# Query sketches on 16 tiles of 32 by 32, half of the first v on ScalarE's queue, five weight casts on GpSimd, and the last 256 queries taken with batch 3

## The chip, the cores and the metric

The kernel runs on one core of a Trainium2 chip. The metric is the device time of one execution in microseconds; the time before is 104.08 us, the median of three runs (103.90 to 104.26). The engines of the core are TensorE (PE; its weight loads are shown apart as PEld), VectorE (DVE), ScalarE (ACT), GpSimd (POOL) and SyncE (SP, which here only issues transfers). All follow fixed instruction orders and wait for each other by semaphores.

## The reference

Two stages follow each other. The first is an attention whose softmax is replaced by a polynomial sketch, for 4 batches, 4 heads, 1088 positions and a head width of 32, with r = 8; the second is a gated feed-forward network (FFN) over 4352 tokens of width 128 with 1536 hidden units.

```python
def phi(x):
    a = np.einsum('rd,bhsd->bhsr', S1, x)
    b = np.einsum('rd,bhsd->bhsr', S2, x)
    return np.einsum('bhsi,bhsj->bhsij', a, b).reshape(*x.shape[:-1], r * r)
q_p, k_p = (phi(q), phi(k))
kv = np.einsum('bhsf,bhsd->bhfd', k_p, v)
z = np.sum(k_p, axis=2)
num = np.einsum('bhsf,bhfd->bhsd', q_p, kv)
den = np.einsum('bhsf,bhf->bhs', q_p, z)[..., None] + 1e-06
x = num / den            # then heads are put side by side: 4352 x 128
gate = np.maximum(x @ w_gate, 0.0)
out = gate * (x @ w_val) @ w_out
```

## The kernel before

**Tokens.** A batch's 1088 positions are 34 columns of 32 tokens. Eight blocks of four such columns (NX = 8) make 1024 tokens; the two columns left over in each batch make one last set of 256 tokens over all four batches. A vector transpose (L1003) turns q into qT, with head and head width on the 128 partitions.

**Keys, class K, once per batch.** kT (L495), the sketches of the keys in TensorE (L502: two groups of 64 rows by four of 32 columns, weights wS, which ScalarE makes at L334), their transposes (L513), the outer products kp on GpSimd (L555; for the first batch one of five pieces on VectorE), z (L528), its masked copy zs (L536), and w (L542), which is z multiplied with S2, so that the denominator of a query needs only a third sketch. ScalarE copies w from PSUM (L547). v is cast to 16 bits by ScalarE (L561); L568 multiplies kp with v, and L575 writes the masked result bz.

**Queries, class Q, in sets.** The sets are: the first 256 tokens of batch 0 (a path of its own, in token order), the next 768 of batch 0, 1024 tokens each of batches 1, 2 and 3, and the last 256. For all but the first, `sk1` (L694) computes the sketches by S1 and S2 of two heads at a time into two PSUM banks, and `sk2` (L701) the third sketch by w into the second half of the first bank. `t2` (L708) and `t2c` (L714) transpose both into SBUF. Small products, a sum and a reciprocal follow (L741, L747, L752, L772). The class G then makes the outer products qqp (L835, on GpSimd), transposes them on TensorE (L853, copied by L858 or L860) or by a transfer (L843), multiplies with bz (L869) and writes xT (L881).

**FFN, class F.** A unit is 512 columns of a gate product (L926), a value product (L938), a relu by ScalarE (L931), a product on VectorE (L948), every sixth one on GpSimd (L943, L953), and the output product (L960), which sums over 12 units of a group of 512 tokens in one bank. Groups follow in the order of the query sets. Weights arrive as nine thirds of 256 KB in fp32 in the buffers of later k, q and v, and are cast to 16 bits by ScalarE (L412) or GpSimd (L414); the dictionary CAST says which.

**Order.** The function issues the early transfers by hand: S1 and S2 on ScalarE's queue, everything else on SyncE's, in the order k0, q0, v0 (four loads of one fourth each), weights, k1, q1. The rest is ordered by a planner (class Plan): each operation has an engine, an estimated cost, what it comes after, the PSUM banks it takes and drops (a Lease of one bank or of two neighbouring ones) and a due time; LAND holds estimated landing times, T0 + u * U the due time of FFN unit u. The planner's times decide only the order in which each engine gets its instructions. Until the FFN starts, dummy matmuls on a zero tile (L320, bank W_BANK = 7) fill TensorE's gaps; that bank joins the others at a planned 11.0 us.

Of the kernel before, what the change touches and what calls it, by code (L numbers as in the profile page):

```python
# [146 lines left out]
def kernel(  # L147
# [79 lines left out]

    nc.scalar.dma_start(out=s16[0:R], in_=S1)
# [6 lines left out]
    nc.sync.dma_start(out=q_sb[0][:, QA:], in_=flat(q, 0)[:, QA:])  # L235
    for a in (0, 2, 1, 3):
        load_v(nc.sync, 0, a)
# [4 lines left out]
    nc.scalar.activation(out=scr, in_=zero[0:1, 0:1], func=ACTF.Relu)  # L242
    W3 = DF // 3
# [57 lines left out]
    NBW = 3  # L301
    bw = [sb([128, NX * H, R + 1], FP32, f"bw{i}") for i in range(NBW)]
    for i in range(NBW):
        nc.vector.memset(bw[i][:, :, R], EPS * DSCALE)
# [6 lines left out]
    nc.vector.tensor_copy(out=sel, in_=id16[:, None, 0:R].to_broadcast([2 * R, 16, R]))  # L311
# [33 lines left out]
    WB = sb([128, 2, H, R], FP32, "WB")  # L345
# [8 lines left out]
    def make_WB():  # L354
        nc.vector.tensor_tensor(
            out=WB, in0=s_t[:, :, None, :].to_broadcast([128, 2, H, R]),
            in1=maskh[:, None, :, None].to_broadcast([128, 2, H, R]), op=ALU.mult)
# [63 lines left out]
    class K:  # L421


        def __init__(self, b, prev):
# [32 lines left out]
            w = P.add("PE", f"w {b}", 0.24, self.w, [self.zc_op, K.l_op], take=[lw])  # L457
            self.wc_op = P.add("ACT", f"wc {b}", 0.15, self.wc, [w], drop=[lw], rec=0.13)
# [135 lines left out]
    class Q:  # L594
# [65 lines left out]
        def places(self):  # L660
# [446 lines left out]
```

## Time and profile before

| what | value |
|---|---|
| median of the runs (three) | 104.08 us |
| the profiled execution, its own time | 104.44 us |
| its span, first to last instruction | 102.5 us |
| PE, PEld busy | 96.9 us (95%), 66.1 us (64%) |
| DVE, ACT, POOL busy | 82.6, 83.2, 60.3 us |
| granted TensorE clock, mean | 0.993 |
| bytes moved | 12.75 MB |
| chain that ended last, by engine | PE 76%, DMA 12%, POOL 3%, ACT 3% |
| chain, L694 and L701 | 2% each |

A row of a group or a timeline names line, engine, operation, the written and the read tile, the shape (partitions x elements) and a count; in brackets stands the idle time of the engine before it and what ended it. The busy time of TensorE includes its pipeline, so that a busy PE is not yet one at its peak. In the chain each piece is the work that the next had to wait for.

### The profile page before, as it was taken

How to read it: one execution, taken by the hardware profiler on the slowest of the kernel's cores; microseconds unless marked ns; L12 is line 12 of the kernel's file. 1: busy time of each engine (PE TensorE's matmuls, PEld its weight loads, DVE VectorE, ACT ScalarE, POOL GpSimd, SP SyncE). 2: the span in 40 equal slices, each digit the busy share in tenths (PEclk: the TensorE clock that was granted, in tenths of full speed). 3: DMA queues.
4: the chain of work that ended last, by engine and by line, in shares of the span. 5: the costliest groups of instructions: out<-in, count | busy, mean ns of one | idle time of the engine just before them, and what ended most of it. 6: DMA issues, size and time to landing. Idle time of an engine off the chain costs nothing.

```text
span 102.5 us, 3040 instructions
## 1 busy us (share of the span) xinstructions
PE 96.9 (95%) x1138; PEld 66.1 (64%) x1138; DVE 82.6 (81%) x178; ACT 83.2 (81%) x167; POOL 60.3 (59%) x64
## 2 busy tenths in 40 slices
PE   6999997999999999999999999999999999999970
PEld 6857995665777465756665746567666566767940
DVE  5789947986898999999998777968758696875960
ACT  3413999979996999889985969899889969999940
POOL 7039259759999179748973985499404419042100
PEclk9999999999999999999999999999999999999997
DMA  2899997299999822400347104005253400240041
GB/s 60 297 284 282 402 414 286 79 196 341 238 244 280 193 77 43 89 0 0 67 89 139 19 6 102 0 0 109 55 101 62 101 7 0 60 94 0 6 97 57
DMA packets 14671, 12.75 MB, mean 124 GB/s; under 512 B 5952, under 2 KB 12352, under 8 KB 14656
## 3 DMA queue, kind: packets, MB, share of 16 engines
q1 hardware_dynamic: 14624, 12.56, 46.7%
q8 instruction: 9, 0.15, 0.6%
q14 instruction: 6, 0.05, 0.2%
q10 hardware_dynamic: 32, 0.00, 0.0%
HBM read 9.14 MB, written 2.23 MB: 111 GB/s over the span
## 4 chain that ended last, share of the span: by engine, by line
PE 76%; DMA 12%; POOL 3%; ACT 3%; SPq 2%; issue 1%; DVE 1%; ACTq 0%
PE ps L960 22%; PE ps L938 21%; PE ps L926 20%; DMA v<-in_moe_w_val_dram 6%; DMA v<-in_v_dram 5%; PE ps L869 3%; PE ps L694 2%; PE ps L701 2%; POOL qqp L835 2%; PE ps L568 2%; PE ps L853 1%; PE ps L502 1%; ACT qpt L860 1%; PE ps L528 1%; ACT g_sb L931 1%
## 5 line engine op out<-in xcount | busy, mean ns | idle before, releaser
L948 DVE TENSOR_TENSOR ht<-g_sb,ps 128x512 f16<-128x512 f16 (+1 forms) x87 | 54.9, 672 | 11.5 <-ACT g_sb L931 9.0
L931 ACT ACTIVATE g_sb<-ps 128x512 f16<-128x512 f32 (+1 forms) x103 | 57.1, 615 | 5.1 <-PE ps L926 3.9
L938 PE MATMUL ps<-xT,wv 128*128 128x512 f16 (+1 forms) x120 | 38.9, 348 | 0.1
L926 PE MATMUL ps<-xT,wg 128*128 128x512 f16 (+1 forms) x120 | 38.7, 347 | 0.0
L960 PEld LDWEIGHTS <-ht 128*128 128x128 f16 x408 | 28.1, 98 | 15.0 <-issue 2.3
L960 PE MATMUL ps<-wo,ht 128*128 128x128 f16 x408 | 36.7, 219 | 1.0 <-POOL wo L414 0.7
L953 POOL TENSOR_TENSOR ht<-g_sb,v_sb 128x512 f16<-128x512 f16 x16 | 18.7, 1167 | 13.6 <-ACT v_sb L943 13.5
L555 POOL TENSOR_TENSOR kp<-kab 128x512 f16<-128x512 f32 (+1 forms) x16 | 18.0, 1154 | 10.6 <-DVE kab L513 10.6
L835 POOL TENSOR_TENSOR qqp<-qan,qab 128x1024 f16<-128x1024 f32 (+1 forms) x9 | 15.8, 1759 | 2.5 <-DVE qan L772 2.2
L938 PEld LDWEIGHTS <-wv 128*128 128x128 f16 x120 | 13.2, 113 | 4.7 <-issue 1.3
L926 PEld LDWEIGHTS <-wg 128*128 128x128 f16 x120 | 13.2, 114 | 3.0 <-issue 0.6
L943 ACT COPY v_sb<-ps 128x512 f32<-128x512 f32 x16 | 9.7, 608 | 0.0
L881 ACT CAST xT<-ps 128x512 f16<-128x512 f32 (+1 forms) x9 | 4.9, 546 | 3.3 <-PE ps L869 3.3
L320 PE MATMUL ps<-zero 128*128 128x128 f16 x70 | 6.7, 264 | 1.0 <-DVE maskkv L295 1.0
L968 ACT ACTIVATE o_sb<-ps 128x512 f32<-128x512 f32 (+1 forms) x10 | 5.6, 564 | 1.3 <-PE ps L960 1.3
L320 PEld LDWEIGHTS <-zero 128*128 128x128 f16 x70 | 5.8, 123 | 1.1 <-DVE maskkv L295 1.0
L495 DVE STREAM_TRANSPOSE kT<-k_sb 128x544 f32<-128x544 f32 (+2 forms) x8 | 5.6, 730 | 0.7 <-DMA k_sb<-in_k_dram 0.7
L1003 DVE STREAM_TRANSPOSE qT<-q_sb 128x576 f32<-128x576 f32 (+4 forms) x10 | 6.0, 613 | 0.2 <-DMA q_sb<-in_q_dram 0.2
L869 PE MATMUL ps<-qpt,bz 128*128 128x512 f16 (+2 forms) x26 | 5.3, 306 | 0.0
L561 ACT CAST v<-v 128x576 f16<-128x576 f32 x8 | 5.0, 679 | 0.2 <-DMA v<-in_v_dram 0.2
L772 POOL TENSOR_TENSOR qan<-qab,qrd 128x256 f32<-128x256 f32 (+1 forms) x4 | 2.2, 545 | 3.9 <-DVE qrd L752 3.9
L568 PEld LDWEIGHTS <-kp 128*128 128x128 f16 (+1 forms) x72 | 3.5, 98 | 1.3 <-issue 0.2
(89 smaller groups left out, 70.9 us busy)
## 6 DMA issues: line engine op xcount, KB each, us to landing
v<-in_v_dram SPq DMA_DIRECT2D x15, 144.0 KB, 6.6
out_dram<-o_sb SPq DMA_DIRECT2D x28, 64.0 KB, 1.8
k_sb<-in_k_dram SPq DMA_DIRECT2D x3, 544.0 KB, 7.1
q_sb<-in_q_dram SPq DMA_DIRECT2D x3, 544.0 KB, 7.9
k_sb<-in_moe_w_out_dram SPq DMA_DIRECT2D x2, 256.0 KB, 6.1
q_sb<-in_q_dram SPq DMA_DIRECT2D x1, 416.0 KB, 5.2
k_sb<-in_k_dram SPq DMA_DIRECT2D x1, 288.0 KB, 2.7
k_sb<-in_k_dram SPq DMA_DIRECT2D x1, 256.0 KB, 3.0
```

The costliest lines, as they stand in the source:

```text
L320: nc.tensor.matmul(PS[:, W_BANK, 0:128], zero, zero, start=True, stop=True)
L555: eng.tensor_tensor(out=self.kp[:, lo:hi].rearrange("p x g (i a c) -> p (x g i) a c", i=2, a=R), in0=src[:, 0, :, :, None].to_broadcast([1 ...
L835: eng.tensor_tensor(out=self.qp[:, lo:hi].rearrange("p x g (i a c) -> p (x g i) a c", i=2, a=R), in0=a_in[:, :, :, None].to_broadcast([128 ...
L869: nc.tensor.matmul(o[:, 0:n * 128].rearrange("f (x t) -> f x t", x=n)[:, :, t], self.ks[b or 0].bz[:, p], self.pt[:, 0:n, p, t], start=(p ...
L926: nc.tensor.matmul(bank(self.lg)[:, y * W:(y + 1) * W], wblock(wg, j), x, start=True, stop=True, skip_group_check=True)
L931: nc.scalar.activation(out=self.gs[:, 0:self.cols], in_=bank(self.lg)[:, 0:self.cols], func=ACTF.Relu)
L938: nc.tensor.matmul(bank(self.lv)[:, y * W:(y + 1) * W], wblock(wv, j), x, start=True, stop=True, skip_group_check=True)
L943: nc.scalar.copy(out=self.vs, in_=bank(self.lv))
L948: nc.vector.tensor_tensor(out=self.ht[:, 0:w], in0=self.gs[:, 0:w], in1=bank(self.lv)[:, 0:w], op=ALU.mult)
L953: nc.gpsimd.tensor_tensor(out=self.ht, in0=self.gs, in1=self.vs, op=ALU.mult)
L960: nc.tensor.matmul(o[:, s], self.ht[:, y * W + s * 128:y * W + (s + 1) * 128], wo[:, j // 4, (j % 4) * DM:(j % 4 + 1) * DM], start=(j == 0 ...
L1003: nc.vector.transpose(qT[b][:, lo * 32:hi * 32], q_sb[b][:, lo * 32:hi * 32])
```

## The change

- **Sketches.** `sk1` and `sk2` become one function `sk`. The weight tile wq holds, for each batch, a block of 32 columns: 8 of S1, 8 of S2, 8 of w and 8 of zeros. Each of four heads (32 rows) and each of four column groups gets its own matmul of 32 by 32 weights, and the heads write to four banks, two leases of two. The two transposes `t2` take a pair of banks each and write one tile abc that has all three sketches. GpSimd adds up the first 16 columns of wq for all batches (`make_wq`); the w part is no longer copied by ScalarE but summed over heads by a VectorE reduction (`wc`). The scaling DSCALE moves into the constant sel.
- **Last 256 queries.** The set of its own is gone. The set of batch 3 has ten blocks instead of eight: the last two are the 256 tokens, with 16 more matmuls of 64 columns, and one chain of small products serves both. Its outer products and transfer transposes stay three groups, the third for the last 256.
- **v of batch 0.** Two of its four loads go on ScalarE's queue, behind a one-element copy of S1's tile (scr2); the second part of q0 moves behind the other two on SyncE's queue.
- **Casts.** ScalarE keeps wg0, wv1 and wg2 and takes wo2; GpSimd has wv0, wg1, wo0, wv2 and wo1.
- **Planner.** New landing times, U = 0.66 for 0.72, bank 7 from a planned 13.0, and no dummy matmuls once an operation has leased bank 7.

Only the places that other tiles and names force are left out of the diff.

```diff
@@ -232,14 +233,18 @@
     nc.sync.dma_start(out=q_sb[0][:, 0:QA], in_=flat(q, 0)[:, 0:QA])
-    nc.sync.dma_start(out=q_sb[0][:, QA:], in_=flat(q, 0)[:, QA:])
-    for a in (0, 2, 1, 3):
-        load_v(nc.sync, 0, a)
     bz = [sb([128, 2, 128], FP16, f"bz{b}") for b in range(B)]
...
     nc.scalar.activation(out=scr, in_=zero[0:1, 0:1], func=ACTF.Relu)
+    scr2 = sb([1, 1], FP32, "scr2")
+    nc.scalar.copy(out=scr2, in_=s16[0:1, 0:1])
+    load_v(nc.scalar, 0, 0)
+    load_v(nc.sync, 0, 2)
+    load_v(nc.scalar, 0, 1)
+    load_v(nc.sync, 0, 3)
+    nc.sync.dma_start(out=q_sb[0][:, QA:], in_=flat(q, 0)[:, QA:])
     W3 = DF // 3
@@ -298,17 +303,19 @@
-    NBW = 3
-    bw = [sb([128, NX * H, R + 1], FP32, f"bw{i}") for i in range(NBW)]
-    for i in range(NBW):
-        nc.vector.memset(bw[i][:, :, R], EPS * DSCALE)
+    QN = [NX, NX + 2, NX]
+    bw = [sb([128, n * H, R + 1], FP32, f"bw{i}") for i, n in enumerate(QN)]
+    for t in bw:
+        nc.vector.memset(t[:, :, R], EPS * DSCALE)
...
-    nc.vector.tensor_copy(out=sel, in_=id16[:, None, 0:R].to_broadcast([2 * R, 16, R]))
+    nc.vector.tensor_scalar_mul(out=sel, in0=id16[:, None, 0:R].to_broadcast([2 * R, 16, R]),
+                                scalar1=DSCALE)
@@ -342,7 +349,10 @@
-    WB = sb([128, 2, H, R], FP32, "WB")
+    WB = sb([128, H, 2, R], FP32, "WB")
+    wq = sb([128, B, 32], FP32, "wq")
+    nc.gpsimd.memset(wq, 0.0)
@@ -353,8 +363,13 @@
-            out=WB, in0=s_t[:, :, None, :].to_broadcast([128, 2, H, R]),
-            in1=maskh[:, None, :, None].to_broadcast([128, 2, H, R]), op=ALU.mult)
+            out=WB, in0=s_t[:, None].to_broadcast([128, H, 2, R]),
+            in1=maskh[:, :, None, None].to_broadcast([128, H, 2, R]), op=ALU.mult)
+    def make_wq():
+        w = wS[:, :, :, None].to_broadcast([128, 2, 2, B, R])
+        nc.gpsimd.tensor_tensor(out=wq[:, :, 0:2 * R].rearrange("p b (w r) -> p w b r", w=2),
+                                in0=w[:, :, 0], in1=w[:, :, 1], op=ALU.add)
@@ -364,10 +379,10 @@
-    P.banks[W_BANK] = 11.0
+    P.banks[W_BANK] = 13.0
...
-    T0, U, SLACK = 11.0, 0.72, 0.25
+    T0, U, SLACK = 11.0, 0.66, 0.25
@@ -388,22 +403,22 @@
-    LAND = {"k0a": 3.6, "S": 4.3, "k0b": 4.25, "q0a": 5.5, "q0b": 7.3, "v0": 9.8,
-            "wg0": 10.2, "wv0": 10.8, "wg1": 11.4, "wv1": 12.0, "wg2": 13.0, "wv2": 13.7,
-            "wo0": 14.3, "wo1": 14.9, "wo2": 15.3,
-            "k1": 17.7, "q1": 19.1, "v1": 23.6, "k2": 27.0, "q2": 29.0, "v2": 32.5,
-            "k3": 35, "q3": 37.5, "v3": 39.0}
+    LAND = {"k0a": 3.6, "S": 4.3, "k0b": 4.25, "q0a": 5.0, "v0": 7.4, "q0b": 8.7,
+            "wg0": 9.35, "wv0": 9.95, "wg1": 10.65, "wv1": 11.3, "wg2": 11.9, "wv2": 12.6,
+            "wo0": 13.25, "wo1": 14.85, "wo2": 15.5, "k1": 16.8, "q1": 18.15, "v1": 23.0,
+            "k2": 26.7, "q2": 28.8, "v2": 32.3, "k3": 34.7, "q3": 37.5, "v3": 39.0}
...
+    wq_op = P.add("POOL", "wq", 0.25, make_wq, [ws_op])
...
-    CAST = {"wg0": "ACT", "wv0": "ACT", "wg1": "ACT", "wv1": "ACT", "wo0": "POOL",
-            "wg2": "ACT", "wv2": "POOL", "wo1": "ACT", "wo2": "POOL"}
+    CAST = {"wg0": "ACT", "wv0": "POOL", "wg1": "POOL", "wv1": "ACT", "wo0": "POOL",
+            "wg2": "ACT", "wv2": "POOL", "wo1": "POOL", "wo2": "ACT"}
@@ -454,8 +469,8 @@
-            w = P.add("PE", f"w {b}", 0.24, self.w, [self.zc_op, K.l_op], take=[lw])
-            self.wc_op = P.add("ACT", f"wc {b}", 0.15, self.wc, [w], drop=[lw], rec=0.13)
+            w = P.add("PE", f"w {b}", 0.16, self.w, [self.zc_op, K.l_op], take=[lw])
+            self.wc_op = P.add("DVE", f"wc {b}", 0.11, self.wc, [w], drop=[lw], rec=0.07)
@@ -543,8 +558,10 @@
         def wc(self):
-            self.wct = sb([128, H * R], FP32, f"wc{self.b}")
-            nc.scalar.mul(out=self.wct, in_=bank(self.lw)[:, 0:32], mul=DSCALE)
+            nc.vector.tensor_reduce(
+                out=wq[:, self.b, 2 * R:3 * R],
+                in_=bank(self.lw)[:, 0:H * R].rearrange("p (h j) -> p j h", h=H), axis=AX.X,
+                op=ALU.add)
 
@@ -623,14 +639,11 @@
-                la = Lease(2)
-                self.la = la
-                s1 = P.add("PE", f"qsk {name}", sk32(cols, 2, 1) + 0.09 if b is not None else 0.61,
-                           lambda: (self.sk1(), self.sk2()), qt1 + wcs, take=[la])
-                t2 = P.add("DVE", f"qt2 {name}", dve(2 * cols), self.t2, [s1] + old, drop=[la],
-                           rec=0.07)
-                t2c = P.add("DVE", f"qt2c {name}", dve(cols), self.t2c, [s1] + old, drop=[la],
-                            rec=0.07)
+                self.l4 = [Lease(2), Lease(2)]
+                s1 = P.add("PE", f"qsk {name}", cols * 0.001667 + 0.19 + 0.05 * (n > NX),
+                           self.sk, qt1 + wcs + [wq_op], take=self.l4)
+                t2, t2c = [P.add("DVE", f"qt2 {name} {i}", dve(2 * cols), lambda i=i: self.t2(i),
+                                 [s1] + old, drop=[self.l4[i]], rec=0.07) for i in range(2)]
@@ -659,15 +672,15 @@
-            if self.b is not None:
-                for a in range(4):
-                    yield (self.b, a,
-                           qT[self.b][:, 0:4 * NX * 32].rearrange("p (x a t) -> p x a t", a=4, t=32)[
-                               :, self.x0:self.x0 + self.n, a],
-                           slice(0, self.n * 32))
-            else:
+            top = min(self.n, NX - self.x0)
+            for a in range(4):
+                yield (self.b, a,
+                       qT[self.b][:, 0:4 * NX * 32].rearrange("p (x a t) -> p x a t", a=4, t=32)[
+                           :, self.x0:self.x0 + top, a], slice(0, top * 32))
+            if self.n > NX:
...
-                    yield b, b, qT[b][:, 4 * NX * 32:NC * 32], slice(0, 64)
+                    yield (b, b, qT[b][:, 4 * NX * 32:NC * 32],
+                           slice(NX * 32, NX * 32 + 64))
@@ -677,42 +690,29 @@
-                    WB.rearrange("p w h r -> p (w h r)"), start=True, stop=True,
+                    WB.rearrange("p h w r -> p (h w r)"), start=True, stop=True,
...
-                out=self.ab[:, :, 0:n].rearrange("p w x h f -> p x w (h f)"),
-                in_=bank(self.la)[:, 0:n * 64].rearrange("p (x w f) -> p x w f", w=2, f=32))
-        def sk1(self):
-            for p in range(2):
-                rows = slice(64 * p, 64 * p + 64)
-                wt = wS[rows].rearrange("p w i r -> p (w i r)")
-                for b, a, src, oc in self.places():
-                    nc.tensor.matmul(
-                        bank(self.la, p)[32 * a:32 * a + 32, oc], wt, src[rows],
-                        start=True, stop=True, skip_group_check=True)
-        def sk2(self):
-            o = bank(self.la)
+                out=self.abc[:, 0:n, :, 0:2 * R],
+                in_=bank(self.la)[:, 0:n * 64].rearrange("p (x h f) -> p x h f", x=n, h=H))
+        def sk(self):
...
-                nc.tensor.matmul(
-                    o[32 * a:32 * a + 32, 256 + oc.start:256 + oc.stop],
-                    (self.ks[0] if self.b is not None else self.ks[b]).wct, src,
-                    start=True, stop=True, skip_group_check=True)
-        def t2(self):
-            b0, b1 = self.la.banks
+                for h in range(H):
+                    r = slice(32 * h, 32 * h + 32)
+                    nc.tensor.matmul(bank(self.l4[h // 2], h % 2)[32 * a:32 * a + 32, oc],
+                                     wq[r, b], src[r], start=True, stop=True,
+                                     skip_group_check=True)
+        def t2(self, i):
+            b0, b1 = self.l4[i].banks
...
-                self.ab[:, :, 0:self.n].rearrange("p w x h f -> p h x w f"),
-                PS[:, b0:b1 + 1:b1 - b0, 0:self.n * 32].rearrange(
-                    "p h (x w f) -> p h x w f", w=2, f=16))
-        def t2c(self):
-            nc.vector.transpose(self.c[:, 0:self.n].rearrange("p x h r -> p (x h r)"),
-                                bank(self.la)[:, 256:256 + self.n * 32])
+                self.abc[:, 0:self.n, 2 * i:2 * i + 2].rearrange("p x h f -> p h x f"),
+                PS[:, b0:b1 + 1, 0:self.n * 32].rearrange("p h (x f) -> p h x f", f=32))
@@ -810,7 +811,7 @@
-            num = P.add("PE", f"num {name}", pe16(2, n * 128) if qs.b is not None else
+            num = P.add("PE", f"num {name}", pe16(2, n * 128) if b is not None else
@@ -1015,20 +1016,22 @@
-    sets = [(0, 0, 2, [(0, 2)]), (0, 2, 6, [(0, 2), (2, 4)])]
-    sets += [(b, 0, NX, [(0, GX), (GX, GX)]) for b in range(1, B)]
-    sets += [(None, 0, 2, [(0, 2)])]
+    sets = [(0, 0, 2, [(0, 0, 2)]), (0, 2, 6, [(0, 0, 2), (0, 2, 4)])]
+    sets += [(b, 0, NX, [(b, 0, GX), (b, GX, GX)]) for b in range(1, B)]
+    sets[-1] = (B - 1, 0, NX + 2, sets[-1][3] + [(None, NX, 2)])
...
-        kk = [ks[b]] if b is not None else ks
-        tt = qt1[b, x0] if b is not None else [qt1[bb, None] for bb in range(B)]
+        kk, tt = [ks[b]], qt1[b, x0]
+        if w > NX:
+            kk, tt = ks, tt + [qt1[bb, None] for bb in range(B - 1)]
...
-        for y, m in parts:
+        for gb, y, m in parts:
...
-            gs.append(G(qq, y, m, i, col, old, TURN[i]))
+            gs.append(G(qq, gb, [ks[gb]] if gb is not None else ks, y, m, i, col, old,
+                        TURN[i]))
@@ -1067,12 +1070,13 @@
     f0 = min(o.start for o in P.ops if o.name.startswith("g "))
-    at = PE0
+    at, kept = PE0, False
     for o in todo:
         if o.eng == "PE":
-            if o.start < f0 + 0.1 and o.start - at > 0.1:
+            if not kept and o.start < f0 + 0.1 and o.start - at > 0.1:
                 warm(int((o.start - at) / (0.107 if o.start < WARM else 0.056)))
             at = o.start + o.busy
+        kept = kept or any(W_BANK in l.banks for l in o.take)
         o.fn()
```

More of the change, by code (lines that the diff above doesn't have):

```diff
@@ L580 @@
     NS, NQ = 3, 3
-    q_ab = [sb([128, 2, NX, 2, 16], FP32, f"qab{i}") for i in range(NS)]
-    q_c = [sb([128, NX, H, R], FP32, f"qc{i}") for i in range(NS)]
-    q_an = [sb([128, NX * H, R], FP32, f"qan{i}") for i in range(NS)]
-    q_dn = [sb([128, NX * H], FP32, f"qdn{i}") for i in range(NS)]
-    q_rd = [sb([128, NX * H], FP32, f"qrd{i}") for i in range(NS)]
+    q_abc = [sb([128, n, H, 4 * R], FP32, f"qabc{i}") for i, n in enumerate(QN)]
+    q_an = [sb([128, n * H, R], FP32, f"qan{i}") for i, n in enumerate(QN)]
+    q_dn = [sb([128, n * H], FP32, f"qdn{i}") for i, n in enumerate(QN)]
+    q_rd = [sb([128, n * H], FP32, f"qrd{i}") for i, n in enumerate(QN)]
     q_qp = [sb([128, GX, 2, 128], FP16, f"qqp{i}") for i in range(NQ)]
@@ L600, in __init__ @@
             i = i % NS
-            self.ab, self.c, self.an = q_ab[i], q_c[i], q_an[i]
+            self.abc, self.an = q_abc[i], q_an[i]
             self.dn, self.rd, self.bw = q_dn[i], q_rd[i], bw[i]
@@ L730, in b_in @@
         def b_in(self):
-            return self.ab[:, 1, 0:self.n].rearrange("p x g (i r) -> p (x g i) r", r=R)
+            return self.abc[:, 0:self.n].rearrange("p x h f -> p (x h) f")[:, :, R:2 * R]
         def mul_ps(self):
@@ L742, in mul @@
                 out=self.bw[:, 0:n * H, 0:R], in0=self.b_in(),
-                in1=self.c[:, 0:n].rearrange("p x h r -> p (x h) r"), op=ALU.mult)
+                in1=self.abc[:, 0:n].rearrange("p x h f -> p (x h) f")[:, :, 2 * R:3 * R],
+                op=ALU.mult)
         def red(self):
@@ L773, in div, with __init__ @@
                 out=self.a_out(),
-                in0=self.ab[:, 0, 0:n].rearrange("p x g (i r) -> p (x g i) r", r=R),
+                in0=self.abc[:, 0:n].rearrange("p x h f -> p (x h) f")[:, :, 0:R],
                 in1=self.rd[:, 0:n * H, None].to_broadcast([128, n * H, R]), op=ALU.mult)
     class G:
-        def __init__(self, qs, x0, n, i, col, old, how):
+        def __init__(self, qs, b, ks, x0, n, i, col, old, how):
             self.qs, self.x0, self.n, self.col = qs, x0, n, col
-            self.ks, self.b = qs.ks, qs.b
+            self.ks, self.b = ks, b
             i = i % NQ
@@ L830, in phi @@
                 assert hi - lo == 1
-                a_in = bank(self.qs.la)[:, y0 * 64:y0 * 64 + 32].rearrange(
-                    "p (y r) -> p y r", r=R)
+                a_in = bank(self.qs.la)[:, y0 * 64:(y0 + 1) * 64].rearrange(
+                    "p (h f) -> p h f", h=H)[:, :, 0:R]
             else:
```

## The prediction

> **What bounds the kernel now.** I read the chain that ended last first, then the busy time of each engine by stretches, then the groups by shape for durations, then the timeline of the first 26 us. From about 24 us to 97 us the chain is TensorE and nothing else, piece behind piece. Around the query sketches of the fourth batch, and of the last 256 tokens, it reads (start, length, what):
>
> ```profile
> 59.82 0.22 PE ps L938
> 60.04 0.59 PE ps L694 x16
> 60.63 0.57 PE ps L701 x8
> 61.20 0.34 PE ps L926
> ...
> 81.75 0.27 PE ps L694 x16
> 82.02 0.25 PE ps L701 x8
> 82.27 0.33 PE ps L960 x4
> ```
>
> The reader is to see that the sketch (L694) and its second part (L701) stand in line with the FFN's matmuls: 0.59 + 0.57 = 1.16 us in which no FFN matmul runs, for each of three full sets, and 0.27 + 0.25 = 0.52 us for the last 256 queries. An FFN unit (gate, value, output) is 0.22 + 0.22 + 0.22 = 0.66 us there. The stretches (length; busy PE, PEld, DVE, ACT, POOL with counts; clock, DMA share, GB/s) show what else is close:
>
> ```profile
> 5.00:7.50 2.50, 2.50 (x43) 1.38 (x42) 2.05 (x9) 0.40 (x2) 0.70 (x1) 1.00 0.98 284
> 10.00:12.50 2.50, 2.50 (x49) 2.13 (x45) 2.43 (x9) 2.35 (x5) 0.95 (x1) 1.00 1.06 406
> ...
> 13.40:20.00 6.60, 5.72 (x72) 5.00 (x77) 4.42 (x8) 6.45 (x14) 5.62 (x6) 1.00 0.63 247
> 25.10:40.00 14.90, 14.90 (x189) 10.04 (x189) 14.19 (x26) 13.50 (x28) 12.09 (x11) 1.00 0.80 196
> 40.00:50.00 10.00, 10.00 (x104) 5.93 (x89) 9.67 (x18) 9.26 (x18) 7.52 (x7) 1.00 0.13 28
> 60.00:70.00 10.00, 10.00 (x98) 5.81 (x98) 7.99 (x15) 8.64 (x18) 6.90 (x7) 1.00 0.13 27
> ```
>
> VectorE is 95 to 97% busy from 25 to 50 us and 80% from 60 on; ScalarE is full from 13.4 to 20; transfers fill the DMA engines from 5 to 15 us. The ramp, from the timeline:
>
> ```profile
> 6.80 4.15 POOL L555 TENSOR_TENSOR kp<-kab 128x512 f16<-128x512 f32 x4 [4.09 <-DVE kab L513]
> 10.14 1.25 ACT L561 CAST v<-v 128x576 f16<-128x576 f32 x2 [0.16 <-DMA v<-in_v_dram]
> 13.11 1.07 POOL L835 TENSOR_TENSOR qqp<-qan,qab 128x512 f16<-128x512 f32 x1 [2.16 <-DVE qan L772]
> 15.04 0.61 POOL L414 CAST wv<-v 128x512 f16<-128x512 f32 x1 [0.86 <-DMA v<-in_moe_w_val_dram]
> 16.21 1.95 POOL L835 TENSOR_TENSOR qqp<-qan,qab 128x1024 f16<-128x1024 f32 x1
> 16.30 0.38 PE L960 MATMUL ps<-wo,ht 128*128 128x128 f16 x4 [0.66 <-POOL wo L414]
> 18.22 0.62 PE L853 MATMUL ps<-ident,qqp 128*128 128x128 f16 x8 [0.22 <-POOL qqp L835]
> ```
>
> The first v and the first key features end together (11.39 and 10.95), the first FFN matmul starts at 13.46, and TensorE then waits for GpSimd (wo cast, qqp) and ScalarE. In 13.4 to 25.1 its useful pieces add up to about 9.3 us (30 + 9 gate and value matmuls of 256 columns at 0.108, 28 of L960 at 0.055, sketches, transposes, features), so some 2.4 us are lost.
>
> **The sketches.** Old: two row groups of 64 by four column groups of 32 (L694), then 128 rows by four (L701). 16 records of L694 take 0.59 us at 256 columns and 0.27 at 64, so 192 columns cost 0.32: 1.67 ns a column, with a fixed part of 0.163. L701 gives (0.57 - 0.25)/192, the same slope, and a fixed part of 0.143 with 8 records: 8 more records cost 0.02. All eight tiles of L694 therefore run at once, in two passes. New: 16 tiles and 32 records, by the same line 0.427 + 0.163 + 16 x 0.0025 = 0.63 us. A set saves 1.16 - 0.63 = 0.53, and two of the full sets do so: 1.06. The third takes the last 64 columns along: 320 columns are 0.533 + 0.20 + about 0.04 for 32 more records = 0.77, against 1.16 + 0.52 = 1.68: 0.91. Together 1.97 us off TensorE. Upper bound: the same. Lower bound: the trace shows only two row groups at a time; if four ran as two after two, a full set would be 2 x 0.427 + 0.20 = 1.05 and the third 2 x 0.533 + 0.24 = 1.31, a saving of 0.22 + 0.37 = 0.59. I take 1.97, since eight tiles already run as one and the four row groups get a bank each.
>
> The Trainium skill, "TensorEngine Tiling (Array Packing)", Instruction Overhead, speaks against it: each matmul has some 60 cycles of overhead, whatever its width. At 2.4 GHz an estimate by that page is 32 x 25 ns = 0.80 us a set and 1.6 us for the third, a saving of only 0.8 us. The trace disagrees as far as it goes: 18 records of L528 are one piece of 0.30 us, under 17 ns each.
>
> **Banks.** The sketch now holds four of eight PSUM banks instead of two, until each transpose of a pair (128x512, 714 ns) is done. What the FFN holds: a gate bank for 1.0 us (matmul at 61.20 to relu's end near 62.2), a value bank for 1.36 (61.54 to the product's end at 62.90), an output bank: (1.0 + 1.36)/0.66 + 1 = 4.6. So 0.6 bank is missing for some 0.6 + 0.7 us. Bounds for the stall a set: nothing, since up to three waiting output matmuls (3 x 0.22 us) need no new bank; and 2 x 0.71 + 0.2 - 0.66 = 0.96 us, if gate and value wait for both transposes. Nothing excludes a gain in VectorE's order, but no row gives one. I take 0.25, as the missing share is small; three sets: +0.75 us.
>
> **VectorE** gets 2 x 714 for 714 + 407 ns, +0.31 a full set and +0.24 in the first batch's set (2 x 583 for 583 + 340), and the column sums of w (nearest row: 128x32, L536, 190 ns) four times. The third set's 640 columns (about 845 ns each, by 131 ns for 128 columns) replace 1.121 + 0.520, and 0.3 of small reductions fall away. ScalarE loses four copies of 198 ns, GpSimd a net 0.34 us of small products. In 25 to 50 us that is +0.5 us on 23.86 of 24.9, just still covered; without that cover each 0.5 would be a stall. It is inside the 0.25 a set and its bound. The new wq sums on GpSimd (nearest row 128x64, 320 ns) fall in the 4.09 us it sits idle before L555 and cost nothing; behind L555's start they would delay it by 0.32.
>
> **v and the queues.** Two of four loads of v move to ScalarE's queue behind a copy that waits for S1, and the last of q moves behind SP's other two. Bytes ahead of v fall by 416 KB, at 284 GB/s 1.5 us: v is whole at about 8.5 instead of 10.0 (bound: 10.0, if ScalarE issues late). The weights keep all those bytes ahead of them. The Trainium skill, "DMA: Bandwidth & Descriptors", Issuing engines are not separate DMA queues, says that a second issuer saves only issue time; the shares of 0.98 and 1.06 above agree, so weights come no sooner. But behind the two issues (v's issues on SP took 1.85 us for four) stands the scaled S (L334): it ran at 4.58 and moves to about 5.1, bounds 4.58 and 5.7 (0.2 for the copy, 0.93 for the issues). On it wait the key sketch (5.31) and L555 (6.80), which ends about 0.5 later, at 11.4. With v early, the key matmuls of the other blocks are done by then and 0.25 us remain: the evacuation that started at 12.14 starts near 11.8. Forecast: first FFN matmul 0.3 earlier; bounds 0.7 earlier (v and features on time) and 0.5 later. The late q is about 1 us later for its set, whose sketch is one step of 0.52 instead of 0.56 + 0.49; L835 stays near 13.1 to 13.6.
>
> **Casts.** ScalarE gives up three casts of 0.63 us and takes one: 1.26 us off an engine that was busy 6.45 of 6.60. GpSimd has five instead of three, +1.22: two fit into its idle 2.16 ahead of L835, or the 1.7 left of it. Its third beyond v's thirds, the middle wo, may stand ahead of the 1.95 us product of the third group and make that 0.61 late. I take 0.4 us of the 2.4 lost back; bounds: 1.2 back (all that ScalarE gives up), 0.6 lost. The changed stop of the warm-up matmuls costs nothing while the granted clock stays at 1.00.
>
> **Sum**, against the profiled execution (104.44 us, span 102.5): -1.97 + 0.75 - 0.3 - 0.4 = -1.92, so 102.52. The median, 104.08, lies 0.36 under that execution, which gives 102.16. Bounds of this case: 100.9 to 103.2.
>
> **Rivals.**
> - *The array does not take 16 tiles at once.* For it: no row has four row groups. Against: eight run as one. Saving 0.59: 104.08 - 0.59 + 0.75 - 0.7 = 103.54. Chance 0.13; the page's 60 cycles would land near there (103.3).
> - *Banks take the place of the sketch, and it is slower.* At each set TensorE needs four free banks in pairs, with VectorE 95% full behind them. It decides from a stall of 1.97/3 = 0.66 us a set; at the bound of 0.96, +2.88 - 1.97 = +0.91, with a ramp that gives nothing 104.99. For it: VectorE's 14.19 of 14.90. Against: 80% from 60 us on, where the third set lies. Chance 0.16.
> - *The ramp gives more.* ScalarE was its limit: -0.7 - 1.2, and no bank stall: 104.08 - 1.97 - 1.9 = 100.2. Against: wo still waits for a transfer that ends near 15. Chance 0.12.
> - *The ramp gives it back*: L334 late (+0.5) and the third group late (+0.6): 104.08 - 1.97 + 0.75 + 1.1 = 103.96. Chance 0.06.
>
> **How the numbers follow.** The forecast has the other 0.53. The range of 100.7 to 104.3 leaves out about half of the slower case and part of the fast one, some 2 in 10; the likeliest's own is 100.9 to 103.2. A measurement tells 0.3%, 0.31 us, from no change. Faster: the forecast, most of the first rival and the third, 0.75; same 0.09, nearly all from the last; slower 0.16.
>
> **What would show it.** In the chain, one piece of about 0.63 us where 0.59 and 0.57 stood, and no pieces at 82; over 0.9 proves the first rival. Idle TensorE, or gate pieces well over 0.22, right behind the sketches with VectorE's transposes as releaser prove the second. L334's start (4.58), the first L561 (10.14), the first L926 (13.46) and the start of the unbroken chain (23.94) show the ramp. The prediction is wrong if the sketches shrink as said and the end does not move, for then TensorE's line was not the limit.

## The result and the profile after

The changed kernel takes 102.50 us (median of six runs, 101.95 to 105.74; the kernel before beside it 104.07): a ratio of 0.9837 [0.9811, 0.9864], 1.6 us less. The profiled execution took 102.43 us, its span is 100.6 us. Ratios and their intervals leave disturbed executions out, so that a median can stand higher than its ratio says; one profiled execution of the experiments, of 532 us, is not read at all.

Many lines moved: the sketch L694/L701 is now L707, its transposes L708/L714 are L713, gate, value and output products L927, L939 and L961, relu L932, VectorE's product L949, GpSimd's casts L429, the outer products of the queries L836, and ScalarE's scaled S L341.

The chain of waits of the changed kernel at its three full sketches, and where the last group's first products stand (start, length, what):

```profile
22.73 0.64 PE ps L707 x32
...
39.06 0.64 PE ps L707 x32
...
57.58 1.11 PE ps L707 x46
58.68 0.33 PE ps L961 x4
59.01 0.23 PE ps L927
59.33 0.60 ACT g_sb L932
59.97 0.38 PE ps L961 x4
...
89.96 0.23 PE ps L870 x8
```

One piece of 0.64 us stands where 0.59 and 0.57 stood, twice; the third, with the last 256 queries in it (each matmul leaves two records, so 64 stand in the trace, 46 of them in this piece of the chain), takes 1.11 us for 1.16 + 0.52; no sketch stands at 82. The sketches give back 0.52 + 0.52 + 0.57 = 1.61 us. L870 of the last group starts at 89.96 us, before at 91.97 us.

Between the first full sketch and this L870 TensorE has the same other work in both kernels: the counts of records differ by one gate product less and four output matmuls more, 0.22 us each way. The stretch takes 91.97 - 23.94 = 68.03 us before and 89.96 - 22.73 = 67.23 us after. That is 0.80 us less, where the sketches alone give 1.61: some 0.8 us are lost there again.

The same stretches as before the change (length; busy PE, PEld, DVE, ACT, POOL with counts; clock, DMA share, GB/s):

```profile
5.00:7.50 2.50, 2.50 (x25) 1.16 (x24) 1.70 (x8) 0.52 (x2) 0.84 (x2) 1.00 1.00 346
10.00:12.50 2.50, 2.50 (x68) 2.08 (x66) 2.00 (x7) 1.03 (x3) 2.29 (x5) 1.00 1.07 403
13.40:20.00 6.60, 6.52 (x87) 5.42 (x85) 6.07 (x12) 5.96 (x13) 4.94 (x5) 1.00 0.44 177
25.10:40.00 14.90, 14.50 (x195) 9.14 (x193) 14.40 (x27) 13.16 (x26) 13.54 (x12) 1.00 0.73 200
40.00:50.00 10.00, 10.00 (x102) 6.66 (x100) 9.96 (x19) 9.73 (x19) 7.20 (x6) 1.00 0.25 55
60.00:70.00 10.00, 10.00 (x94) 6.34 (x94) 8.31 (x15) 9.66 (x20) 8.33 (x7) 1.00 0.27 60
```

Three things differ. From 13.4 to 20 TensorE is busy 6.52 of 6.60 us (before 5.72). From 25.1 to 40 it has 0.40 us idle, where it had none. VectorE, at 14.19 and 9.67 before, now has 14.40 of 14.90 and 9.96 of 10.00 us: it is full. The chain there leaves TensorE:

```profile
27.58 0.64 DVE ht L949
28.26 0.38 PE ps L961 x4
...
34.31 0.45 PE ps L939 x2
34.85 0.69 DVE ht L949
35.64 0.49 DVE qT L1004
36.25 0.67 DVE qT L1004
36.92 0.58 DVE ht L949
37.50 1.14 ACT g_sb L932 x2
38.68 0.38 PE ps L961 x4
```

From 34.85 us on VectorE's queue sets the pace: two transposes of later queries (L1004) stand between two FFN products, ScalarE's relu (L932) comes late behind them, and TensorE's next output product waits for that relu until 38.68 us. Between 20 and 44 us the chain before had no VectorE piece.

By the starts of its matmuls, TensorE has three waits here that the kernel before has not: 0.35 us ahead of 28.26 us, with VectorE's L949 as the releaser, and 0.38 and 0.25 us ahead of 38.68 and 59.97 us, with the relu as the releaser. Each time it is the first output product of a new group that waits, after 48, 96 and 192 of the 408 output matmuls, the one that opens the group's bank. Its weights, the hidden values, are loaded already (at 27.85, 38.24 and 59.51 us), so it doesn't wait for them; its other operand, wo, was cast by 19.3 us. What is left is the bank, which the releaser has just read; that is inferred, as the trace leaves out the numbers of the banks. The first two waits lie ahead of the second sketch. The third lies behind the third sketch, while VectorE's transposes of that sketch (58.69 to 60.27 us) still hold its four banks. Right behind the second and the third sketch, at 39.71 and 58.68 us, an FFN matmul follows at once.

The ramp, from the timeline (start, busy, engine, line; in brackets the idle time before and its releaser):

```profile
2.13 0.87 ACTq L216 DMA_DIRECT2D v<-in_v_dram  x2
4.35 0.44 ACT L341 ACTIVATE wS<-ps,maskp 128x16 f32<-128x16 f32 x2 [1.11 <-PE ps L333]
6.92 4.15 POOL L572 TENSOR_TENSOR kp<-kab 128x512 f16<-128x512 f32 x4 [1.66 <-DVE kab L528]
7.36 1.24 ACT L578 CAST v<-v 128x576 f16<-128x576 f32 x2
11.42 1.05 DVE L713 STREAM_TRANSPOSE qabc<-ps 128x384 f32<-128x384 f32 x2 [0.47 <-PE ps L707]
12.38 0.61 POOL L429 CAST wv<-v 128x512 f16<-128x512 f32 x1 [0.20 <-DMA v<-in_moe_w_val_dram]
12.39 0.25 DVE L592 TENSOR_TENSOR bz<-ps,maskkv 128x128 f16<-128x128 f32 x1
12.56 0.64 DVE L741 TENSOR_TENSOR bw<-qabc 128x192 f32<-128x192 f32 x1
14.01 0.38 PE L927 MATMUL ps<-xT,wg 128*128 128x256 f16 x2
14.63 2.98 POOL L836 TENSOR_TENSOR qqp<-qan,qabc 128x512 f16<-128x512 f32 x2 [0.95 <-DVE qan L773]
```

ScalarE's queue issues its two loads of v at 2.13 us, while its table load runs (1.67 to 2.95 us); the copy of S1's tile, which stands ahead of them in the kernel's text, runs at 3.07. So S is not held up (4.35, before 4.58). v is cast from 7.36 (before 10.14), and the last value third of the weights from 12.38 (before 15.04). Yet the first FFN matmul starts at 14.01 us, later than the 13.46 of before: on VectorE, L592, which writes bz, stands behind the transposes of the second set's sketch (11.42 to 12.47), and xT follows behind L741.

### The profile page after: what moved, and what is told of

Same layout as the page of the kernel before. It is cut to its first block, busy times and chain, and to the rows that moved or that the text cites. A ratio compares the mean times of both kernels' runs of the same rounds, so it can differ in the third digit from the quotient of the medians.

```text
span 100.6 us, 3136 instructions
## 1 busy us (share of the span) xinstructions
PE 95.8 (95%) x1188; PEld 66.0 (66%) x1188; DVE 83.8 (83%) x178; ACT 82.0 (81%) x162; POOL 61.5 (61%) x66
## 4 chain that ended last, share of the span: by engine, by line
PE 85%; DVE 7%; ACT 3%; issue 1%; DVEq 0%; ACTq 0%
PE ps L961 22%; PE ps L927 21%; PE ps L939 20%; PE ps L327 5%; PE ps L870 4%; PE ps L517 3%; PE ps L707 3%; ACT g_sb L932 3%; DVE ht L949 3%; PE ps L585 2%; PE ps L854 2%; DVE qT L1004 1%; DVE qabc L713 1%; PE ps L543 1%; PE ps L718 1%
## 5 line engine op out<-in xcount | busy, mean ns | idle before, releaser
L949 DVE TENSOR_TENSOR ht<-g_sb,ps 128x512 f16<-128x512 f16 (+1 forms) x87 | 55.6, 671 | 9.3 <-PE ps L939 4.3
L932 ACT ACTIVATE g_sb<-ps 128x512 f16<-128x512 f32 (+1 forms) x103 | 57.6, 609 | 6.4 <-PE ps L927 5.7
L961 PEld LDWEIGHTS <-ht 128*128 128x128 f16 x408 | 28.4, 98 | 17.1 <-POOL ht L954 3.6
L927 PE MATMUL ps<-xT,wg 128*128 128x512 f16 (+1 forms) x120 | 38.5, 347 | 0.1
L961 PE MATMUL ps<-wo,ht 128*128 128x128 f16 x408 | 37.2, 219 | 0.7 <-ACT g_sb L932 0.2
L939 PE MATMUL ps<-xT,wv 128*128 128x512 f16 (+1 forms) x120 | 36.4, 347 | 0.0
L954 POOL TENSOR_TENSOR ht<-g_sb,v_sb 128x512 f16<-128x512 f16 x16 | 18.7, 1167 | 18.2 <-ACT v_sb L944 8.0
L836 POOL TENSOR_TENSOR qqp<-qan,qabc 128x1024 f16<-128x1024 f32 (+1 forms) x9 | 15.7, 1759 | 1.2 <-DVE qan L773 1.0
L927 PEld LDWEIGHTS <-wg 128*128 128x128 f16 x120 | 13.4, 113 | 3.4 <-issue 1.1
L939 PEld LDWEIGHTS <-wv 128*128 128x128 f16 x120 | 13.3, 114 | 3.6 <-issue 0.2
L327 PE MATMUL ps<-zero 128*128 128x128 f16 x80 | 7.7, 259 | 1.0 <-DVE maskkv L300 1.0
L327 PEld LDWEIGHTS <-zero 128*128 128x128 f16 x80 | 6.4, 119 | 1.1 <-DVE maskkv L300 1.0
L1004 DVE STREAM_TRANSPOSE qT<-q_sb 128x576 f32<-128x576 f32 (+4 forms) x10 | 5.8, 604 | 0.0
L713 DVE STREAM_TRANSPOSE qabc<-ps 128x512 f32<-128x512 f32 (+2 forms) x8 | 5.2, 689 | 0.5 <-PE ps L707 0.5
L870 PE MATMUL ps<-qpt,bz 128*128 128x512 f16 (+2 forms) x26 | 5.3, 306 | 0.0
L585 PE MATMUL ps<-v,kp 128*128 128x64 f16 (+1 forms) x72 | 4.5, 193 | 0.0
```

What stands on the lines that cost most here:

```text
L327: nc.tensor.matmul(PS[:, W_BANK, 0:128], zero, zero, start=True, stop=True)
L836: eng.tensor_tensor(out=self.qp[:, lo:hi].rearrange("p x g (i a c) -> p (x g i) a c", i=2, a=R), in0=a_in[:, :, :, None].to_broadcast([128 ...
L870: nc.tensor.matmul(o[:, 0:n * 128].rearrange("f (x t) -> f x t", x=n)[:, :, t], self.ks[b or 0].bz[:, p], self.pt[:, 0:n, p, t], start=(p ...
L927: nc.tensor.matmul(bank(self.lg)[:, y * W:(y + 1) * W], wblock(wg, j), x, start=True, stop=True, skip_group_check=True)
L932: nc.scalar.activation(out=self.gs[:, 0:self.cols], in_=bank(self.lg)[:, 0:self.cols], func=ACTF.Relu)
L939: nc.tensor.matmul(bank(self.lv)[:, y * W:(y + 1) * W], wblock(wv, j), x, start=True, stop=True, skip_group_check=True)
```

## The experiments

Twelve kernels ran, in three groups, each beside runs of the kernel before (104.41, 104.26 and 104.07 us). Unless another is named, the edit is made to the changed kernel.

### Which half of the change pays: sketches alone, ramp alone

e1_sketch_only is the changed kernel with the old order of transfers, old LAND and old CAST; e2_ramp_only is the kernel before with the new ones. LAND goes with them. The edit of e1 (that of e2 is its reverse, on the kernel before):

```diff
-    scr2 = sb([1, 1], FP32, "scr2")
-    nc.scalar.copy(out=scr2, in_=s16[0:1, 0:1])
-    load_v(nc.scalar, 0, 0)
-    load_v(nc.sync, 0, 2)
-    load_v(nc.scalar, 0, 1)
-    load_v(nc.sync, 0, 3)
     nc.sync.dma_start(out=q_sb[0][:, QA:], in_=flat(q, 0)[:, QA:])
+    for a in (0, 2, 1, 3):
+        load_v(nc.sync, 0, a)
...
-    CAST = {"wg0": "ACT", "wv0": "POOL", "wg1": "POOL", "wv1": "ACT", "wo0": "POOL",
-            "wg2": "ACT", "wv2": "POOL", "wo1": "POOL", "wo2": "ACT"}
+    CAST = {"wg0": "ACT", "wv0": "ACT", "wg1": "ACT", "wv1": "ACT", "wo0": "POOL",
+            "wg2": "ACT", "wv2": "POOL", "wo1": "ACT", "wo2": "POOL"}
```

> The changed kernel with the old transfer order, the old landing times and the old casts; sketches on 16 tiles and the last 256 queries with batch 3 stay. Theory: the sketches save 0.52 us twice and 0.57 once (pieces of 1.16 and 0.52 us before, 0.64 and 1.11 after), 1.6 us in sum, of which VectorE gives some 0.5 us back as waits between 26 and 42 us: 1.0 to 1.6 us below before, 102.5 to 103.1 us. Rival: the new ramp carries the gain and the sketches give everything back to VectorE: within 0.3 us of before, near 104.0 us.

> The kernel before with the new transfer order, landing times and casts, sketches as before. Theory: the thirds of the weights land some 2 us earlier and the waits of TensorE before 25 us go (about 1.0 us), while the start of the FFN may move by half a microsecond either way: 0.4 to 1.2 us below before, 102.9 to 103.7 us. Rival: the gain needs the shorter sketches, since the ramp's order is set by VectorE: within 0.3 us of before.

e1: 0.989 [0.9839, 0.9941], which is 1.1 us of 104; the theory held. Sketches and merged queries carry most of the gain. e2: 1.0067 [1.0027, 1.0106], slower: theory and rival both missed. The profile of e2 is of an execution with a low clock from 9 to 13 us (it is shown in the last section), but that isn't all: of its runs with a mean clock of 0.999 or more three took 104.29, 104.85 and 104.97 us (a fourth, of 107.49, is left out), the kernel before at the same clock, in the same group, 103.83 to 104.95, median 104.24. On the old sketches the new ramp brings nothing.

### v on one queue

```diff
-    load_v(nc.scalar, 0, 0)
+    load_v(nc.sync, 0, 0)
     load_v(nc.sync, 0, 2)
-    load_v(nc.scalar, 0, 1)
+    load_v(nc.sync, 0, 1)
```

> The changed kernel with all four loads of the first v on SyncE's queue, in the same order, ahead of the last part of q. Theory: two queues are what moved more bytes (326 to 362 GB/s between 2.5 and 10 us against 268 to 301 before), since loads of two groups of 32 partitions then run side by side: the last third of the value weights lands 1 us or more later than at 12.38 and the time rises by 0.3 to 1.0 us. Rival: the order alone did it: landing within 0.4 us of 12.38 and the same time within 0.3 us.

0.9907 [0.9876, 0.9939] against the 0.9837 of two queues. In its profile v is cast at 8.42 us (two queues: 7.36) and the last value third at 14.79 (12.38). That favours two queues. But e4 below, with the transfers of the changed kernel, had v at 8.92 and the third at 14.31 us, so one execution with one queue proves little: how fast the early bytes come differs between executions with the same transfers. The times lean to two queues, though e4's 0.9877, also with two, lies inside the interval of e3; by what mechanism stays open.

### bz of the first batch ahead of the second set's transposes

```diff
                 t2, t2c = [P.add("DVE", f"qt2 {name} {i}", dve(2 * cols), lambda i=i: self.t2(i),
-                                 [s1] + old, drop=[self.l4[i]], rec=0.07) for i in range(2)]
+                                 [s1] + old + ([ks[0].kve] if b == 0 else []), drop=[self.l4[i]],
+                                 rec=0.07) for i in range(2)]
```

> The changed kernel, only that VectorE gets the masked key result bz of batch 0 ahead of the two transposes of the second query set. Theory: bz stood behind these transposes (key matmuls done at 11.66, bz at 12.39), and the small product that followed ran next to a cast on GpSimd: the first FFN matmul moves from 14.01 to about 13.3 to 13.5 and the time falls by 0.3 to 0.6 us against the changed kernel. Rival: the ramp is limited behind it by GpSimd's outer products, which now come later: the first FFN matmul moves, the time stays within 0.3 us.

0.9877 [0.9835, 0.9919]: no gain. The theory that the late bz costs the ramp its time fell. In that execution the first FFN matmul came at 15.01 us, since q came later and xT stood behind the same transposes and small products, now placed ahead of it.

### The changed kernel once more

> The changed kernel, on the chip and beside the runs of the other kernels of this group. Theory: the landing of the early transfers differs from execution to execution (the kernel with the masked key result first has the same transfers, yet its first v was whole at 8.9 us and the last third of the value weights at 14.3, against 7.4 and 12.4), and the FFN's start follows it: 102.2 to 102.9 us, and the landing times say how much of the ramp's gain is the change's own. Rival: the landings are those of the first profile again (7.4 and 12.4, within 0.3 us), so that the later ones belong to that kernel.

0.9834 [0.9785, 0.9883]. v is cast at 7.81 us and the last value third at 12.44. Sketches at 22.79, 39.12 and 57.64 us, L870 of the last group at 90.02, first FFN matmul at 14.06: the shape of the first profile, and not of e4. It is the profile that the next ones are read against.

### The old casts

```diff
-    CAST = {"wg0": "ACT", "wv0": "POOL", "wg1": "POOL", "wv1": "ACT", "wo0": "POOL",
-            "wg2": "ACT", "wv2": "POOL", "wo1": "POOL", "wo2": "ACT"}
+    CAST = {"wg0": "ACT", "wv0": "ACT", "wg1": "ACT", "wv1": "ACT", "wo0": "POOL",
+            "wg2": "ACT", "wv2": "POOL", "wo1": "ACT", "wo2": "POOL"}
```

> The changed kernel with the old list of casts, six on ScalarE and three on GpSimd. Theory: ScalarE is full in the ramp, so three casts more of 0.63 us cost 0.4 to 1.0 us. Rival: VectorE's order and the transfers set the ramp and GpSimd's free time is worth as much as ScalarE's: within 0.3 us of the changed kernel.

0.9875 [0.9809, 0.9941], span 100.6 us as with the new casts. Who casts the weights can't be told from nothing here; the interval is wide enough that the theory's 0.4 us isn't excluded either.

### The third sketch: its short matmuls first

```diff
-            for b, a, src, oc in self.places():
+            for b, a, src, oc in sorted(self.places(), key=lambda p: p[3].stop - p[3].start):
```

> The changed kernel with the 16 matmuls of 64 columns ahead of the 16 of 256 in the sketch of batch 3. Theory: the second group waits for the tiles of the first, and its weight loads do not overlap: the piece took 1.11 us against 0.64 for one group, 0.47 for 64 columns; with the short group first the long one's loads wait only for 64 columns: 0.9 to 1.0 us. Rival: each group pays its fixed part, whatever the order: 1.1 us again. The time is within 0.3 us of the changed kernel either way; the trace decides.

0.9856 [0.9795, 0.9917]. The third sketch in its chain:

```profile
57.54 1.10 PE ps L707 x53
```

With 1.10 us for 1.11 the order changes nothing: the theory, that a long second group can load its weights early, fell. A second group of 16 matmuls on the same 16 tiles adds 1.11 - 0.64 = 0.47 us for 64 columns, of which the slope of 1.67 ns explains 0.11. The rest, some 0.35 us, is a fixed part that the group pays again, larger than the first group's 0.64 - 0.427 = 0.21; why it is larger stays open. The run settled a second point by chance: its first FFN matmul came at 13.20 us, 0.86 earlier than in c1, and its sketches at 22.70, 39.03 and 57.54 and its span of 100.6 us are within 0.1 us of those there. GpSimd's first two L836 end at 17.7 us in both, and the chain goes on from there.

### 16 tiles at once, or eight after eight

```diff
-                s1 = P.add("PE", f"qsk {name}", cols * 0.001667 + 0.19 + 0.05 * (n > NX),
-                           self.sk, qt1 + wcs + [wq_op], take=self.l4)
+                s1 = [P.add("PE", f"qsk {name} {i}", cols * 0.001667 + 0.16 + 0.05 * (n > NX),
+                            lambda i=i: self.sk(i), qt1 + wcs + [wq_op], take=[self.l4[i]])
+                      for i in range(2)]
...
-                for h in range(H):
+                for h in (2 * i, 2 * i + 1):
```

Here the same 16 matmuls (32 records) go out as two groups of eight tiles, each with its own two banks. e11_halves_sa_first has the edit of e9, below, as well.

> The changed kernel, with each query sketch as two groups of eight tiles, two banks each, one after the other. Theory: the gain of the sketches is that 16 tiles run at once: two pieces of 0.59 us for one of 0.64, so TensorE gets 0.54 us back twice and 0.3 to 0.6 us in the third set: 1.0 to 1.6 us slower than the changed kernel. Rival: four banks at once cost what the shorter sketch saves, and with two at a time FFN matmuls run between the halves: within 0.4 us of the changed kernel.

> The sketch in two groups of eight tiles, two banks each, as tried before, with SA and WB first, so that the clock should stay at 1.00. Theory: pieces of about 0.6 us twice for one of 0.64, 1.0 to 1.6 us slower than the changed kernel: 103.4 to 104.1 us. Rival: most of what the halves lost before was the fall of the clock: within 0.5 us of the changed kernel.

e7: 0.9943 [0.9905, 0.9981], profiled in an execution with a low clock early on; e11: 0.9964 [0.9935, 0.9993], at a clock of 1.00 in the early stretches where e7's fell; both theories held. The sketches of e11 in its chain:

```profile
23.51 0.90 PE ps L708 x32
39.28 1.14 PE ps L708 x32
58.66 1.40 PE ps L708 x53
...
91.19 0.23 PE ps L871 x8
```

0.90 + 1.14 + 1.40 = 3.44 us against 0.64 + 0.65 + 1.10 = 2.39 us in e9, which is the same kernel with the sketches whole: 1.05 us more, and L871 of the last group starts 0.80 us later than there (90.39). The same sketch takes 0.90 at the first place and 1.14 at the second, so a piece can hold a wait too. So the gain of the sketches rests on 16 tiles running together: as eight after eight they give back 0.9964 - 0.9874, or 0.9 us of the 1.3 that e9 is ahead of the kernel before.

### SA sooner, and the place of GpSimd's products

In three more kernels VectorE writes SA and WB, the weights that the first 256 queries need on TensorE, before it transposes the first queries (L1004); in e2 and e7 TensorE had waited for SA at 6.6 us. e8_ramp_sa_first does so on e2, e9_sa_first on the changed kernel; e10_pool_fifth also gives GpSimd every fifth FFN product, where every sixth was its own.

```diff
-    qt1[0, 0] = [t1(0, 0, 8, land["q0a"])]
+    qt1[0, 0] = [t1(0, 0, 8, land["q0a"], [sa_op, wb_op])]
...
-    pool_units = set(range(4, n_units - 3, 6))
+    pool_units = set(range(4, n_units - 3, 5))
```

> The kernel before with the new transfer order, landing times and casts (as in the run of the ramp alone), and with VectorE making the masked sketch weights SA and WB ahead of the transpose of the first part of q. Theory: in the run of the ramp alone TensorE stood idle for 0.31 us at 6.3 us for SA, behind a late transpose, and the granted clock fell to 0.50 from 9.3 to 12.7 us, so that the first FFN matmul came at 16.17; without the idle time the clock stays at 1.00 and the ramp is worth 0.2 to 0.8 us: 103.3 to 104.0 us. Rival: the ramp alone is slower for its order of work, not for the clock: 104.4 to 105.0 us again with a clock of 1.00.

> The changed kernel with SA and WB ahead of that transpose. Theory: the late clock falls go, and the undisturbed time stays within 0.3 us of the changed kernel (102.3 to 102.8 us), since the FFN's start does not set the end. Rival: the earlier product of S moves the whole ramp: 0.3 us or more below it.

> As the changed kernel with SA and WB first, and GpSimd taking every fifth FFN product instead of every sixth: four products of 0.62 us less on VectorE, four copies of 0.61 more on ScalarE. Theory: VectorE, 97% busy from 25 to 50 us, holds TensorE up there (the chain passes through it from 34.9 to 37.5 us): 0.3 to 1.0 us below the changed kernel. Rival: ScalarE, about as full, becomes the limit, or the banks are: no better, 0 to 0.8 us slower.

e8: 1.0104 [1.0067, 1.0141], slower again, and 104.39 and 104.98 us at a mean clock of 1.00: the rival held. Writing SA sooner does not mend the ramp on the old sketches; the cause stays open. e9: 0.9874 [0.9854, 0.9895], no gain, as its theory had it. e10: 0.9882 [0.9859, 0.9906], no gain either: its theory missed. Its chain behind the first full sketch, at the second one, and at the end:

```profile
24.17 0.68 DVE qabc L713
...
24.86 0.52 ACT g_sb L932
...
25.42 0.38 PE ps L939
...
38.50 0.64 PE ps L707 x32
...
89.50 0.23 PE ps L870 x8
...
95.03 0.55 ACT v_sb L944
...
95.69 1.20 POOLq L1106
...
96.94 0.88 PE ps L961 x12
```

The piece at L1106, a line outside the kernel's function, is GpSimd's queue while L954 runs. The VectorE pieces of 34.85 to 36.92 us are gone from this chain, and the second sketch comes 0.62 us earlier than in c1. But nothing is won by that: between the first two full sketches TensorE does four output matmuls, one gate and one value product fewer than in c1, 0.65 us of work. By the third sketch as much is done as in c1, and it starts at 57.63 us (c1: 57.64). Instead TensorE waits 0.31 us right behind the first sketch, ahead of the value product at 25.42, and the chain leads from there over a relu back to VectorE's transpose of that sketch (L713), which is close to the sign that the prediction named for the banks.

Between the third sketch and the last group e10 gains something: the wait of 0.25 us behind the third sketch isn't there, and L870 starts 0.52 us earlier than in c1 with 0.22 us of output matmuls less done, so 0.3 us are won. At the end it is lost again: this edit puts a GpSimd product near the last unit, where it takes 1.16 us (95.72 to 96.88), with ScalarE's copy of 0.55 ahead of it, for the 0.70 us of VectorE's L949 that stands there in the changed kernel, and the last L961 wait for it. So e10 shows the price of a GpSimd product in the wrong place. It doesn't show what VectorE's load costs the changed kernel. Every fifth product without one at the end was not tried.

## Why the prediction was right, and where its steps were not

The median, 102.50 us, lies 0.34 above the forecast of 102.16 and inside the forecast's own range. The terms, against what was measured:

| term | forecast | measured | shown by |
|---|---|---|---|
| sketches and last queries | -1.97 | -1.61 | pieces of the chain |
| stalls from the change | +0.75 | about +0.8 | first full sketch to the last L870, less the sketches |
| both together | -1.22 | -0.8 to -1.1 | the same stretch; e1 |
| ramp | -0.7 | -0.5 to -1.0 | the whole against e1; start of the first full sketch |

**Sketches.** The forecast of 0.63 us for a full set was met (0.64): 16 matmuls (32 records) on 16 tiles run as one step of two passes. The Trainium skill, "TensorEngine Tiling (Array Packing)", Instruction Overhead, has some 60 cycles of overhead for each matmul; added up over the 32 records that gave an estimate of 0.80 us, and the 0.64 us of the trace do not bear out that sum. The rival by which the array does not take 16 tiles is refuted by the piece and by e11, which does to the kernel what that rival supposed. The step that failed is the third set: 0.77 was forecast, 1.11 measured, since I took the slope from 64 to 256 columns of one group to hold for 64 more columns in a second group. The second group pays a fixed part of its own, in either order (e6). This term was 0.34 too good.

**Stalls.** The size was right, 0.8 us for 0.75, but partly by luck. The prediction saw TensorE wait for banks behind each sketch, since the transposes hold four of them. A wait for a bank is what the trace shows, by inference, but only one of the three, of 0.25 us, lies behind a sketch (in e10 one of 0.31 us lies behind the first). The two larger ones, 0.35 and 0.38 us, lie ahead of the second sketch, where no sketch holds a bank: there VectorE's L949 and, behind VectorE's queue, the relu give a bank back late. The prediction costed VectorE's added work at +0.5 us, "just still covered" between 25 and 50 us, and so put it at nothing; it was not covered. How much each cause takes stays open, since e10, which was to tell, moved work about instead. As a rival, the banks needed a stall of 0.66 us a set and a slower kernel: that is refuted, at 0.8 us for all three sets.

**Ramp.** The sum is near, its steps were wrong. ScalarE's two issues do not hold up the scaled S: 5.1 was forecast, 4.35 measured, as they go out beside the table load. Weights were to come no sooner; the last value third came 2.6 to 2.7 us sooner in both profiles of the changed kernel, though in e4, with the same transfers, only 0.7. The first FFN matmul was to come 0.3 earlier; it came 0.55 later, and e6 shows that this point sets nothing, as GpSimd's L836 end at 17.7 either way. The casts were to give 0.4; e5 finds nothing that can be told from zero, nor from 0.4. What is left, 0.9837 and 0.9834 against e1's 0.989, is about 0.5 us, but e1's interval reaches down to 0.9839. L870 of the last group starts at 90.48 us in e1 and at 89.96 and 90.02 with the new ramp, which agrees. The first full sketch starts at 22.73 us, before at 23.94, with 0.22 us of FFN matmuls less done, so 1.0 us sooner. By the same count e1 loses some 0.5 us behind it, the changed kernel 0.8: part of what the ramp wins is lost again. On the old sketches the same ramp costs time (e2, e8); why is not settled.

**The sum.** By the two profiles: the first full sketch 1.0 us sooner at equal work, -1.61 in the sketches, +0.8 lost behind them, and 0.1 us less behind the last L870, in all -1.9, as the spans say (102.5 and 100.6 us). The forecast for the profiled execution was -1.92 and 102.52 us; it took 102.43. That this is so close is luck in part: the sketches were 0.36 too good, the ramp 0.3 too dear. The 0.34 by which the median misses comes from the forecast's last step, which took off 0.36 since the profiled execution of before lay that much above its median; the changed kernel's lies 0.07 below its own. So part of the 1.0 us of ramp in this pair may be a slow ramp in that one execution; the runs don't tell.

## What to carry to other kernels

Matmuls that fill a part of the array are worth putting side by side on all 16 tiles: time goes by the columns and a fixed part, not by the count; but a second group on the same tiles pays the fixed part again, so one longer group should be better than a short one more (that was not tried). When work moves to an engine that is nearly full, look for its cost in what that engine's queue makes late, which can lie elsewhere than where the work was added. A landmark that comes sooner proves nothing until the work done before it is counted: in e10 a sketch came 0.62 us sooner because 0.65 us of work had gone behind it. A start that looks late costs nothing if a later step has another limit, so look for that step before moving the start.

## What the runs showed of the hardware

**A clock at half speed after a short idle time.** Stretches of e2, e7 and e11 from 5 us on (length; busy PE, PEld, DVE, ACT, POOL with counts; clock, DMA share, GB/s), first e2:

```profile
5.00:7.50 2.50, 2.19 (x22) 0.80 (x21) 1.61 (x7) 0.12 (x1) 0.34 (x1) 1.00 0.97 290
...
9.00:11.00 2.00, 2.00 (x26) 2.00 (x26) 1.93 (x7) 1.69 (x5) 2.00 (x3) 0.66 1.09 391
11.00:13.00 2.00, 2.00 (x32) 0.83 (x29) 0.14 (x1) 0.00 (x0) 1.43 (x3) 0.50 1.01 386
```

e7:

```profile
5.00:7.50 2.50, 2.06 (x22) 0.74 (x20) 1.52 (x6) 0.11 (x1) 0.60 (x2) 1.00 0.97 325
...
9.00:11.00 2.00, 2.00 (x24) 2.00 (x22) 1.97 (x9) 1.14 (x4) 2.00 (x3) 0.60 0.99 334
```

e11:

```profile
5.00:7.50 2.50, 1.98 (x25) 0.94 (x23) 1.81 (x9) 0.38 (x1) 1.10 (x2) 1.00 1.04 315
...
9.00:11.00 2.00, 2.00 (x55) 1.90 (x65) 1.97 (x9) 1.27 (x4) 2.00 (x3) 1.00 1.05 398
```

In e2 and e7 TensorE was idle for 0.31 and 0.44 us between 5 and 7.5 us, up to its start at 6.64 and 6.65 us. A granted clock of 0.66 and 0.60 over the two microseconds from 9 on means half speed from about 9.6 and 9.4 us, some 3 us after the idle time, and it lasted for about 3 us. In e11 it was idle for 0.52 us there and the clock stayed at 1.00. So the idle time alone does not bring the fall; what else it takes stays open.

**Two engines at SBUF.** VectorE's L741, which reads two operands from SBUF, took 0.34 us before the change, in e3 and in e5, each time with GpSimd idle, but 0.64 in the changed kernel and 0.46 in c1, each time beside a GpSimd cast that had started earlier and ended while it ran. In e10, where L741 started first (12.42 us, the cast 12.58), it took 0.34. The Trainium skill, "SBUF — State Buffer", Who interferes with whom, says that a VectorE instruction with two SBUF inputs contends with a GpSimd instruction that reads SBUF, through a shared pair of ports that one of them locks; these rows agree.
